# Threshold attention with a feed-forward layer: turning q on VectorE in blocks of 32 from batch 2 on, and spreading inverted sums by DMA

## The chip, the cores and the metric

The kernel runs on one core of a Trainium2 chip. The metric is the device time of one execution in microseconds (us); runs of the same kernel are compared by their median. One execution was taken with the hardware profiler, and its trace is what the views of the profile are read from.

The core's engines run side by side, each through its own instructions in order: TensorE (PE in the profile, with PEld for its weight loads), VectorE (DVE), ScalarE (ACT), GpSimd (POOL) and SyncE (SP). SP computes nothing here; it issues DMAs. An engine waits on semaphores for what another engine or a DMA must have done first.

## The reference

```python
def _attn_ref(q, k, v, tau):                       # q, k, v: 8 batches, 8 heads, 576 tokens, 64
    scale = 1.0 / np.sqrt(q.shape[-1])
    scores = scale * np.matmul(q, k.transpose(0, 1, 3, 2))
    thresh = np.max(scores, axis=-1, keepdims=True) - tau
    scores = np.where(scores >= thresh, scores, -1000000000.0)
    scores = scores - np.max(scores, axis=-1, keepdims=True)
    attn = np.exp(scores)
    attn = attn / (np.sum(attn, axis=-1, keepdims=True) + 1e-09)
    return np.matmul(attn, v).astype(np.float32)

def _moe_ref(x, w_in, w_out):                      # x: 4608 x 512, d_ff = 2048
    h = x @ w_in
    g = np.maximum(0.01 * h, h)
    return (g @ w_out).astype(np.float32)
```

The attention's output, with the heads side by side, is x. Inputs and the output are float32. tau is 0.02, and only scores within tau of the row's maximum count.

## The kernel before

**Tiling.** A *pair* p is two heads of one batch: 32 pairs, four to a batch. A *couple* c is two pairs: 16 couples. A couple's scores are made in nine *steps* t: steps 0 to 3 are 128 query rows each of its first pair, 4 to 7 of its second, and step 8 holds the last 64 rows of both. Each step has two tiles of 128 x 576, one for each head of the pair (h = 0, 1). The program's outer loop goes over 17 values of c and 9 of t, and the last c only finishes the work of couple 15.

**One step.** `s_mm` (L159) makes both score tiles as three fp16 products each (q and k are split into a high part `hi` and a remainder `lo`). They go into the PSUM tag `s`, which has two buffers of two banks, one for each head, so the next step's scores need both to have been read. `s_max` reads a tile with VectorE (L182: scales, negates, takes the minimum, writes `sn`), GpSimd adds tau (L187, `nth`), and then there are two ways to the masked exponentials W. In the plain way ScalarE makes the exponentials `e` (L192), and VectorE masks and sums them (L215, called by `s_mask` a step later). In the *direct* way ScalarE does it all, with two activations (L198, L202). `s_mask` also issues a transposing DMA of W into `wT` from SP (L221). W has six buffers.

**Preparing q and k.** `load_qk` loads a pair's q (L81: one DMA of 256 KB, in pieces of 256 B; L86: the last 64 rows) and k into `nat`, three buffers. `prep(p, i)` turns them so that the 64 head elements lie on partitions: i = 0 is q, four fp32 transposes of 128 x 128 on TensorE (L130) into the PSUM tag `A`; i = 1 is k and both tails, five. ScalarE then copies PSUM to `hi` (L139), and VectorE makes `lo` (L140). Four preparations belong to a couple.

**Sums.** A couple's 18 columns of sums are inverted (`sums_0`, L229; `sums_1`, L235), split into two fp16 parts (L236, and `sums_2`, L241), turned into rows by one product (`sums_3`, L247) and copied by ScalarE (L250). `sums_4` spreads the rows over the partitions of the output tile by products with a selection matrix, five for e = 0 and six for e = 1 (L264), and ScalarE copies each result to `rc` (L269). `values` (L280) multiplies `wT` with v, and VectorE multiplies by `rc` and writes x (L290).

**Feed-forward.** When a batch's x is there, `push_main` puts 32 *units* into a list: 16 of w_in (`h_unit`, L302, each followed by a ScalarE activation, L306) and 16 of w_out (`out_mm`, L317; every fourth is evicted by ScalarE, L328, and every second eviction is followed by a store from SP, L350). The last 64 rows of two batches are collected for `push_tail`, twice four units. The units are independent of the couple in progress and fill TensorE between the other steps.

**Order.** The order within a step is written by hand as a string of words for each t. `share` says which part of the waiting units a step gets, `ahead_of` how many of them run early in the step, and the tiles that go the direct way depend on c, t and whether the step's units hold one of w_in. The instructions of each engine are issued in exactly this order.

Of the kernel before, what the change touches and what calls it, by code (L numbers as in the profile page):

```python
# [9 lines left out]
FP32 = mybir.dt.float32  # L10
# [6 lines left out]
def kernel(  # L17
# [24 lines left out]
    sb = ctx.enter_context(tc.tile_pool(name="sb", bufs=1))  # L42
    ps = ctx.enter_context(tc.tile_pool(name="ps", bufs=1, space=bass.MemoryType.PSUM))
# [29 lines left out]
    def load_qk(p, i, tail):  # L73

        b, g = divmod(p, NG)
        if p not in nat:
            nat[p] = sb.tile([128, 9, 2, 64], FP32, tag="nat", bufs=3, name="nat")
        t = nat[p]
        h2 = (q, k)[i][b, 2 * g:2 * g + 2, :, :]
        if not tail:  # L80
            nc.sync.dma_start(  # L81
                out=t[0:128, 4 * i:4 * i + 4, :, :],
                in_=h2[:, 0:512, :].rearrange("h (p c) d -> p c h d", c=4),
            )
        else:
            nc.sync.dma_start(  # L86
                out=t[ds(64 - 64 * i, 64), 8, :, :],
                in_=h2[:, 512:576, :].rearrange("h p d -> p h d"),
            )
# [22 lines left out]
    due = []  # L112

# [9 lines left out]
    def prep(p, i, tag="A", bufs=1):  # L123
# [3 lines left out]
        pt = pair_of_banks(tag, bufs).rearrange("p a b -> p (a b)")  # L127
        for c in range(4 + i):
# [10 lines left out]
        due.append(lambda: nc.scalar.activation(out=hi[:, :], in_=pt[:, 0:N], func=AF.Copy, bias=0.0, scale=QS))  # L139
        soon.append(lambda: nc.vector.scalar_tensor_tensor(  # L140
            out=lo[:, :], in0=pt[:, 0:N], scalar=QS, in1=hi[:, :],
            op0=OP.mult, op1=OP.subtract,
        ))
        qk.setdefault(p, {})[i] = (hi, lo)

    def s_mm(c, t):
# [17 lines left out]
        sc[(c, t)] = out  # L164

    live, dens = {}, {}

    def s_max(c, t, h, direct):
# [3 lines left out]
        if t == 0 and h == 0:  # L172
            dens[c] = sb.tile([128, 18], FP32, tag="den", bufs=2, name="den")
        if h == 0:
# [20 lines left out]
        else:  # L195
# [8 lines left out]
                accum_out=dens[c][:, 2 * t + h:2 * t + h + 1],  # L204
            )

    def s_mask(c, t):
# [5 lines left out]
        for h in range(2):  # L213
            if h not in masked:
# [3 lines left out]
                    accum_out=dens[c][:, 2 * t + h:2 * t + h + 1],  # L218
                )
        q0 = 512 if t == 8 else t * 128 + (t // 4) * 128  # L220
# [4 lines left out]
    def sums_0(c):  # L225

# [6 lines left out]
    def sums_1(c):  # L233
        d1, rr = inv[c]
        nc.vector.reciprocal(out=rr[:, :], in_=d1[:, :])  # L235
        nc.gpsimd.tensor_scalar(out=r2[:, 0, 0:18], in0=rr[:, :], scalar1=1.0 / RS, scalar2=0.0,  # L236
                                op0=OP.mult, op1=OP.add)

    def sums_2(c):
        d1, rr = inv[c]  # L240
        nc.vector.scalar_tensor_tensor(out=r2[:, 1, 0:18], in0=rr[:, :], scalar=1.0 / RS, in1=r2[:, 0, 0:18],  # L241
                                       op0=OP.mult, op1=OP.subtract)

    def sums_3(c):

# [6 lines left out]

    def sums_4(c, e):

        row = rows[c]
# [12 lines left out]
        rc = sb.tile([128, 576], FP32, tag="rc", bufs=2, name="rc")  # L268
        due.append(lambda: nc.scalar.activation(out=rc[:, :], in_=t[:, 0:576], func=AF.Copy, bias=0.0, scale=1.0))  # L269
        rcs[e] = rc  # L270

    def values(c, e):
# [12 lines left out]
        rc = rcs.pop(e)  # L285
# [3 lines left out]
        def mul():  # L289
            nc.vector.tensor_tensor(  # L290
# [45 lines left out]
    def push_main(b):  # L336

# [3 lines left out]
        for u in range(2):  # L341
# [7 lines left out]
            def store(o, u=u):  # L349
                nc.sync.dma_start(  # L350
                    out=out[ds(b * S, 512), :].rearrange("(p c) n -> p c n", c=4)[:, 2 * u:2 * u + 2, :],
                    in_=o[:, :, :],
                )
# [26 lines left out]
    with tc.manual_schedule():  # L380
# [15 lines left out]
        for p in range(1, 3):  # L396
# [8 lines left out]
        share = (20, 21, 23, 13, 20, 13, 26, 29, 26)  # L405
        ahead_of = (3, 3, 1, 3, -1, 1, 1, 1, -1)

        plain = "scores first units turn_qk evict spread evict second more mask soon"
        before = "scores turn_qk evict first second mask soon"
        orders = {  # L410
            0: "scores turn_qk evict units first second more mask soon",
            1: "scores invert first units rest more second mask soon",
            3: "scores values first units second more mask soon",
            5: "scores first values units second more mask soon",
            6: "scores first turn_qk evict units more second mask soon",
            8: "scores first units turn_qk evict more second mask soon",
        }
# [3 lines left out]
        for c in range(NC + 1):  # L421
            last = c == NC
            for t in range(NT):
                step = c * NT + t
                if c > 1 and c % 2 == 0 and t == 6:

                    if c % 4 == 2 and c > 2:
# [6 lines left out]
                nxt = {6: (2 * c + 2, 0), 7: (2 * c + 2, 1), 8: (2 * c + 3, 0), 0: (2 * c + 1, 1)}  # L434
                if c == 0:
                    nxt[0], nxt[1] = (1, 0), (1, 1)
                pi = nxt.get(t)
                if pi is not None and pi[0] >= NP:
                    pi = None

                ahead = [share[i % NT] for i in range(step, (c // 2 * 2 + (0 if c % 2 == 0 and t < 6 else 2)) * NT + 6)]
                credit = min(credit, 1.0) + (len(units) - credit) * share[t] / sum(ahead)
                n = min(int(credit + 0.01), len(units))
                credit -= n
                n1 = min(n, (n + ahead_of[t]) // 2)
                direct = tau_f <= 16.0 and (
                    t not in (0, 1, 3) if c < 3 else t in (2, 5, 7, 8) or not any(u[0] for u in units[:n]))
                direct0 = tau_f <= 16.0 and c < 3 and t in (0, 3, 5)

                if c == 0 and t < 2 or c < 2 and t == 6:  # L450
                    order = before
                else:
                    order = orders.get(t, plain)
                    if c == 1 and t == 0:
                        order = "scores first turn_qk evict second mask soon"
                for part in order.split():
                    if part == "scores" and not last:
                        s_mm(c, t)
                    elif part == "values" and c > 0:
                        values(c - 1, t // 2 - 1)  # L460
                    elif part == "first" and not last:
                        s_max(c, t, 0, direct0)
                    elif part == "second" and not last:
                        s_max(c, t, 1, direct)
                    elif part == "invert" and c > 0:
                        sums_1(c - 1)
                    elif part == "rest" and c > 0:
                        sums_2(c - 1)
                    elif part == "units":
                        work(n1)  # L470
                    elif part == "more":
                        if c > 0 and t == 1:
                            work(n - n1 - 1)
                            sums_3(c - 1)
                            work(1 if n > n1 else 0)
                        else:
                            work(n - n1)
                    elif part == "turn_qk" and pi is not None:
                        prep(*pi)
                    elif part == "spread" and c > 0 and t in (2, 4):  # L480
                        sums_4(c - 1, t // 2 - 1)
                    elif part == "evict":
# [56 lines left out]
```

## Time and profile before

| | |
|---|---|
| median of 3 runs | 529.51 us (528.81 to 530.55) |
| the profiled execution | 528.58 us |
| its span | 526.8 us |
| mean granted TensorE clock | 0.969 |
| DMA packets, bytes | 266813, 80.50 MB |
| packets under 512 B | 251904 |
| HBM read, written | 36.70 MB, 9.44 MB |

The span is the stretch from the first to the last instruction that was profiled. Busy times of an engine are the union of its instructions; instructions of VectorE and ScalarE overlap their successors by some 0.08 us, so a group's mean is a little more than what one instruction adds. In the lines shown below, L12 is line 12 of the kernel. DMA share is the time that packets took, as a share of 16 DMA engines, summed over the queues, and can pass 1.

### The profile page before, as it was taken

What the parts mean: (1) busy time and instruction counts of PE and PEld (TensorE: products, weight loads), DVE (VectorE), ACT (ScalarE), POOL (GpSimd) and SP (SyncE); (2) the same over time, 40 slices, a digit from 0 to 9 for tenths busy, and PEclk for the clock granted to TensorE, in tenths of its full rate; (3) what the DMA queues carried; (4) which work ended last, traced back from release to release, by engine and by line L of the source; (5) the groups of instructions that cost most, each with busy time, mean ns of one, the idle gap of its engine ahead of it and who ended that gap; (6) DMA issues with size and microseconds to landing.
All of it is one profiled execution on the core that took longest, in us unless ns stands there. A gap on an engine that the chain in (4) does not pass through costs nothing.

```text
span 526.8 us, 12333 instructions
## 1 busy us (share of the span) xinstructions
PE 494.7 (94%) x4384; PEld 272.9 (52%) x4384; DVE 414.7 (79%) x1076; ACT 444.0 (84%) x795; POOL 186.4 (35%) x430
## 2 busy tenths in 40 slices
PE   5577787999999999999999999999999999999996
PEld 3344444555555566555555566555555565545444
DVE  5878887998899888998899888998899888982000
ACT  3896979989999899989898999989898999983622
POOL 0754446543443234323443234323433244321000
PEclk9786969999999999999999999999999999999999
DMA  6999999998997899887999689887998799853011
GB/s 154 137 164 184 205 186 198 206 183 175 164 186 145 152 173 168 167 142 165 183 170 142 150 176 188 146 138 156 189 164 152 147 169 154 116 85 93 40 41 60
DMA packets 266813, 80.50 MB, mean 153 GB/s; under 512 B 251904, under 2 KB 264192, under 8 KB 266752
## 3 DMA queue, kind: packets, MB, share of 16 engines
q1 hardware_dynamic: 249136, 70.68, 75.0%
q0 software_dynamic: 17536, 8.92, 14.8%
q8 instruction: 34, 0.56, 0.5%
q14 instruction: 27, 0.22, 0.1%
q10 hardware_dynamic: 80, 0.13, 0.1%
HBM read 36.70 MB, written 9.44 MB: 88 GB/s over the span
## 4 chain that ended last, share of the span: by engine, by line
PE 83%; ACT 7%; DVE 5%; issue 2%; DMA 2%; POOL 0%; SPq 0%; DVEq 0%; ACTq 0%; POOLq 0%
PE u L317 24%; PE u L302 22%; PE s L159 21%; PE A L280 8%; PE A L130 6%; DVE sn L182 3%; ACT W L202 2%; ACT far L198 2%; ACT e L192 2%; PE A L264 1%; DMA nat<-in_q_dram 1%; DVE W L215 1%; DMA nat<-in_k_dram 1%; ACT hi L139 1%; ACT gM L306 0%
## 5 line engine op out<-in xcount | busy, mean ns | idle before, releaser
L182 DVE TENSOR_SCALAR_CACHE_REDUCE sn<-s 128x576 f32<-128x576 f32 x288 | 207.6, 754 | 41.9 <-PE s L159 40.2
L187 POOL TENSOR_SCALAR nth<-nmx 128x1 f32<-128x1 f32 x288 | 125.6, 436 | 242.2 <-DVE sn L182 219.1
L192 ACT ACTIVATE e<-sn,nmx 128x576 f16<-128x576 f32 x181 | 137.6, 770 | 17.6 <-DVE sn L182 16.4
L215 DVE SCALAR_TENSOR_TENSOR W<-sn,nth,e 128x576 f16<-128x576 f32 x181 | 144.3, 814 | 0.0
L302 PE MATMUL u<-xT,win 128*128 128x512 f16 x512 | 122.7, 380 | 0.4 <-ACT gM L306 0.4
L317 PE MATMUL u<-wout,gM 128*128 128x512 f16 x512 | 122.1, 380 | 0.0
L159 PEld LDWEIGHTS <-hi 64*128 64x128 f16 (+1 forms) x1280 | 65.9, 99 | 70.4 <-issue 53.4
L159 PE MATMUL s<-hi,hi 64*128 64x288 f16 x512 | 87.6, 300 | 11.4 <-DVE sn L182 9.7
L159 PE MATMUL s<-hi,lo 64*128 64x288 f16 (+1 forms) x640 | 93.1, 294 | 0.0
L159 PE MATMUL s<-lo,hi 64*128 64x288 f16 (+1 forms) x640 | 92.8, 293 | 0.0
L198 ACT ACTIVATE far<-sn,nth 128x576 f32<-128x576 f32 x107 | 82.5, 771 | 8.2 <-POOL nth L187 6.3
L302 PEld LDWEIGHTS <-win 128*128 128x128 f16 x768 | 61.2, 98 | 52.5 <-issue 8.4
L202 ACT ACTIVATE W<-far,ntau 128x576 f16<-128x576 f32 x107 | 83.0, 775 | 3.5
L306 ACT ACTIVATE gM<-u 128x512 f16<-128x512 f32 x128 | 71.5, 590 | 6.8 <-PE u L302 6.8
L317 PEld LDWEIGHTS <-gM 128*128 128x128 f16 x512 | 46.5, 98 | 52.6 <-issue 7.9
L140 DVE SCALAR_TENSOR_TENSOR lo<-A,hi 128x512 f16<-128x512 f32 (+1 forms) x63 | 47.6, 755 | 17.0 <-ACT hi L139 16.6
L130 PE MATMUL A<-I,nat 128*128 128x128 f32 x283 | 45.9, 291 | 10.4 <-DVE lo L140 5.1
L139 ACT ACTIVATE hi<-A 128x512 f16<-128x512 f32 (+1 forms) x63 | 40.0, 636 | 10.1 <-PE A L130 10.1
L280 PE MATMUL A<-wT,V 128*64 128x288 f16 x640 | 48.0, 298 | 0.0
L130 PEld LDWEIGHTS A<-I,nat 128*128 128x128 f32 x283 | 32.1, 145 | 26.0 <-DVE lo L140 13.8
L280 PEld LDWEIGHTS <-V 128*64 128x64 f16 x640 | 35.1, 113 | 11.7 <-issue 8.0
L328 ACT ACTIVATE osb<-u 128x512 f32<-128x512 f32 x35 | 20.6, 590 | 23.7 <-PE u L317 23.7
(44 smaller groups left out, 302.8 us busy)
## 6 DMA issues: line engine op xcount, KB each, us to landing
nat<-in_q_dram SPq DMA_DIRECT2D x32, 256.0 KB, 3.6
nat<-in_k_dram SPq DMA_DIRECT2D x32, 256.0 KB, 3.8
out_dram<-osb SPq DMA_DIRECT2D x16, 512.0 KB, 3.6
wT<-W SPq DMA_TRANSPOSE x144, 4.1
V<-in_v_dram POOLq DMA_DIRECT2D x8, 256.0 KB, 5.7
win<-in_moe_w_in_dram POOLq DMA_DIRECT2D x16, 128.0 KB, 5.2
V<-in_v_dram POOLq DMA_DIRECT2D x16, 128.0 KB, 4.9
wout<-in_moe_w_out_dram POOLq DMA_DIRECT2D x16, 128.0 KB, 4.7
```

The source lines that it names most:

```text
L130: nc.tensor.matmul(out=pt[0:128, ds(c * 128, 128)], lhsT=t[0:128, 4 * i + c, :, :].rearrange("p h d -> p (h d)"), rhs=I32[:, :], is_transp ...
L159: nc.tensor.matmul(out=out[h][po, half, 0:288], lhsT=qk[p][i][a][r, cols], rhs=qk[p][1][b][r, ds(half * 288, 288)], start=(ti == 0), stop= ...
L182: nc.vector.tensor_scalar(out=sn[:, h, :].rearrange("p (a b) -> p a b", a=2), in0=s_[:, :, 0:288], scalar1=-BS, scalar2=None, op0=OP.mult, ...
L187: nc.gpsimd.tensor_scalar(out=nth[:, h:h + 1], in0=nmx[:, h:h + 1], scalar1=1.0, scalar2=tau_f, op0=OP.mult, op1=OP.add,)
L192: nc.scalar.activation(out=e[:, h, :], in_=sn[:, h, :], func=AF.Exp, bias=nmx[:, h:h + 1], scale=-1.0,)
L198: nc.scalar.activation(out=far[:, :], in_=sn[:, h, :], func=AF.Prelu, bias=nth[:, h:h + 1], scale=-1.0, alpha=BIG,)
L202: nc.scalar.activation(out=w[:, ds(h * 576, 576)], in_=far[:, :], func=AF.Exp, bias=ntau[:, 0:1], scale=1.0, accum_out=dens[c][:, 2 * t + ...
L215: nc.vector.scalar_tensor_tensor(out=w[:, ds(h * 576, 576)], in0=sn[:, h, :], scalar=nth[:, h:h + 1], in1=e[:, h, :], op0=OP.is_le, op1=OP ...
L280: nc.tensor.matmul(out=t[ds(h * 64, 64), half, 0:288], lhsT=vb[:, g, h, kb, :], rhs=wT[:, 4 * h + kb, ds(e * 576 + half * 288, 288)], star ...
L302: nc.tensor.matmul(out=t[:, ts(j, N)], lhsT=w_in16[:, gi, ts(j0 + j, 128)], rhs=xs[gi], start=(gi == 0), stop=(gi == NG - 1), skip_group_c ...
L306: nc.scalar.activation(out=g_out, in_=t[:, 0:nj * N].rearrange("p (j n) -> p j n", j=nj), func=AF.Prelu, bias=0.0, scale=1.0, alpha=0.01)
L317: nc.tensor.matmul(out=t[:, :], lhsT=g_in(j), rhs=w_out16[:, j, :], start=(j == 0), stop=(j == NJ - 1), skip_group_check=True,)
```

## The change

1. **q of pairs 8 to 31** (batch 2 and later) is loaded by four DMAs of 64 KB, in pieces of 128 B, so that block (h, e) of 32 head elements lies on partitions 64 h + 32 e and after, and 32 rows times 16 token blocks in the free dimension. One VectorE instruction then transposes all 32 x 32 blocks into an SBUF tile `qT`. `hi` and `lo` are made from that tile. The query rows of these pairs come out in another order, and the main stores of batches 2 to 7 undo it: four DMAs for each store of one.
2. **Inverted sums of couples 3 to 14** are turned in fp32 by one TensorE transpose, copied by ScalarE to a tile of 18 x 128, written to DRAM by one DMA (`sums_d`) and read back by four DMAs (`sums_b`), each of which broadcasts one half row of 640 elements over 64 partitions into `rc`. The split into two fp16 parts, the eleven products of `sums_4` and the two copies by ScalarE are left out for them. Couples 0, 1, 2 and 15 keep the products.
3. **New orders**, shares and choices of direct tiles: five lists of nine orders, for c = 0, 1, 2, for odd c from 3 on and for even c from 4 on. In the last two the values stand in steps 5 and 6 instead of 3 and 5, and a batch's units are pushed at step 7 instead of 6.

In the orders S is the scores, 0 and 1 are the tiles' `s_max`, M the mask and transposing DMA of the tile before, U, u and w are units, Pa to Pe are preparations (Pa and Pc are q of the next couple's pairs, Pb and Pd k), h runs the ScalarE copies that are due, L the VectorE work that is due, d, r, x, T, D, R, Q are the steps of the sums (D the row to DRAM, R the broadcast), V is the values, and G pushes units.

```diff
+        if i == 0 and not tail and b >= 2:
+            tq = t[0:128, 0:4, :, :].rearrange("p c h d -> p (c h d)")
+            for h in range(2):
+                for e in range(2):
+                    nc.sync.dma_start(
+                        out=tq[ds(64 * h + 32 * e, 32), :].rearrange("r (b d) -> r b d", d=32),
+                        in_=h2[h, 0:512, ds(32 * e, 32)].rearrange("(r b) d -> r b d", r=32),
+                    )
+            return
...
-        pt = pair_of_banks(tag, bufs).rearrange("p a b -> p (a b)")
-        for c in range(4 + i):
+        turn = i == 1 or p < 2 * NG
+        if turn:
+            pt = pair_of_banks(tag, bufs).rearrange("p a b -> p (a b)")
+        else:
+            pt = sb.tile([128, 512], FP32, tag="qT", bufs=2, name="qT")
+            nc.vector.transpose(
+                out=pt[:, :].rearrange("p (t b r) -> p b t r", t=4, b=4),
+                in_=t[0:128, 0:4, :, :].rearrange("p c h d -> p (c h d)").rearrange("p (b t r) -> p b t r", t=4, b=4),
+            )
+        for c in range(4 + i if turn else 0):
...
+    def by_dma(c):
+        return 3 <= c < 15
...
     def sums_3(c):
+        if by_dma(c):
+            d1, rr = inv[c]
+            t = pair_of_banks().rearrange("p a b -> p (a b)")
+            nc.tensor.matmul(out=t[0:18, 0:128], lhsT=rr[:, :], rhs=I32[:, :], is_transpose=True,
+                             skip_group_check=True)
+            row = sb.tile([18, 128], FP32, tag="row32", bufs=2, name="row32")
+            due.append(lambda: nc.scalar.activation(out=row[:, :], in_=t[0:18, 0:128], func=AF.Copy, bias=0.0, scale=1.0))
+            rows[c] = row
+            return
...
+    def sums_d(c):
+        d = dr.tile([18, 128], FP32, tag="dr", bufs=2, name="dr")
+        nc.sync.dma_start(out=d[:, :], in_=rows[c][:, :])
+        rows[c] = d
+
+    def sums_b(c):
+        d = rows[c]
+        for e in range(2):
+            rc = sb.tile([128, 640], FP32, tag="rc", bufs=2, name="rc")
+            src = d.rearrange("(h i) q -> h (i q)", h=2)[:, ds(512 * e, 640)]
+            for h in range(2):
+                nc.sync.dma_start(out=rc[ds(64 * h, 64), :], in_=src[h:h + 1, :].to_broadcast([64, 640]))
+            rcs[e] = rc[:, ds(64 * e, 576)]
...
+                    for x in range(4):
+                        nc.sync.dma_start(
+                            out=rows_.rearrange("(r x c) n -> x r c n", x=4, c=4)[x, :, 2 * u:2 * u + 2, :],
+                            in_=o[ds(32 * x, 32), :, :],
+                        )
...
-        share = (20, 21, 23, 13, 20, 13, 26, 29, 26)
+        share = (17, 24, 26, 13, 17, 16, 23, 38, 23, 17, 24, 29, 13, 17, 16, 23, 38, 23)
```

The two lists of orders from c = 3 on, one line for each step:

```
odd c                          even c
S Pd h w U 0 h 1 u M d L       S Pd h w U 0 h 1 u M d L
S r 0 U x T u 1 h D w L M      S r 0 U x T u w h D 1 M L
S 0 U Q0 h w u 1 M L R         S 0 U Q0 h w 1 M L u R
S U 0 1 u M L w                S 0 U 1 u w M L
U S 0 Q1 h 1 L M w u           U S 0 Q1 h 1 L M Pa h w u
S V0 0 U w 1 L Pa h M u        S V0 0 U w 1 L M h u
S V1 0 G h U 1 u M L           w S V1 0 h U 1 u M L
S Pc 0 U Pb h 1 u M L          G S Pc 0 U Pb h 1 u M L
S 0 U h u 1 M L w              S 0 U h u 1 M L
```

Q does nothing where the sums go by DMA, and G nothing in odd c. Direct tiles from c = 3 on: h = 0 at step 5 alone; h = 1 at steps 2, 5 and 8, in even c at 3 too, and otherwise, at steps 4 and 6 (in even c 0, 4 and 6), where none of the step's units is of w_in.

## The prediction

> **What bounds the kernel now.** I read the engines' totals first, then the busy time couple by couple, then the chain of waits inside a couple, then the prices, and last the DMA queue of SP. A couple c is 18 score tiles (9 steps); its borders below are the starts of its first `sn`.
>
> ```profile
> PE 494.7 (94%) x4384; PEld 272.9 (52%) x4384; DVE 414.7 (79%) x1076; ACT 444.0 (84%) x795; POOL 186.4 (35%) x430
> ```
>
> The page's totals make TensorE the first suspect, but they average a start, a middle and an end. The table by stage (length, then busy us of PE, PEld, DVE, ACT, POOL, granted clock, DMA share, GB/s) shows couple 2 and then couples 8, 9, 10 and 11:
>
> ```profile
> 65.40:94.78 29.38, 24.23 (x216) 14.37 (x216) 23.94 (x63) 26.28 (x50) 16.61 (x36) 0.85 1.30 196
> 240.60:270.10 29.50, 29.50 (x263) 15.74 (x264) 24.84 (x65) 27.33 (x52) 12.28 (x27) 1.00 1.04 174
> 270.10:299.55 29.45, 29.45 (x263) 15.83 (x264) 26.88 (x70) 26.48 (x47) 8.92 (x22) 1.00 0.83 145
> 299.55:329.11 29.56, 29.56 (x311) 17.92 (x312) 24.84 (x64) 27.50 (x52) 12.27 (x27) 1.00 1.11 190
> 329.11:358.57 29.46, 29.46 (x263) 15.83 (x264) 27.66 (x73) 26.97 (x49) 8.93 (x22) 1.00 0.81 138
> ```
>
> From couple 4 on every couple lasts 29.5 us and PE is busy in all of it. DVE has 4.7 us to spare in even couples but only 1.8 to 2.6 in odd ones, ACT 2.1 to 3.0. So a microsecond off PE is a microsecond off the time only until DVE's spare time is used up, and the change gives DVE more work. In couples 0 to 2 no engine is full. The chain of waits inside couples 8 and 9 prices the PE work (start, us, piece):
>
> ```profile
> 252.65 0.36 PE A L264 x6
> ...
> 259.60 0.58 PE A L130 x4
> ...
> 266.85 0.64 PE A L130 x4
> ...
> 275.16 0.06 PE A L247
> ...
> 277.02 0.25 PE A L264 x5
> ```
>
> L130 x4 is the turn of one q, L264 x5 and x6 the two spreads of a couple, L247 the turn of the sums.
>
> **PE.** By the change's conditions q is turned on DVE for pairs 8 to 31, 24 turns: 24 x 0.60 = 14.4 us leave PE. The spreads of couples 3 to 14 go: 12 x (0.36 + 0.25) = 7.3 us. The turn of the sums becomes an fp32 transpose, 0.15 (a quarter of 0.60) for 0.06: 12 x 0.09 = 1.1 us come back. The net is 20.6 us. A couple from 4 to 14 would need 29.49 - 1.20 - 0.61 + 0.09 = 27.8 us of PE. The profiled execution took 528.58 us (span 526.8, 1.8 around it), so with PE always fed it would take 508.0. The Trainium skill (VectorE: DVE Perf Modes, The three transpose paths) gives 390 ns for one 128x128 TensorE transpose and 311 ns for VectorE; 96 at 390 ns would be an estimated 37 us. The chain shows 0.15 us each, and the trace decides.
>
> **DVE, ACT.** The prices, with mean ns of one:
>
> ```profile
> L140 DVE SCALAR_TENSOR_TENSOR lo<-A,hi 128x512 f16<-128x512 f32 x32 | 22.0, 688 | 6.3 <-ACT hi L139 6.0
> L192 ACT ACTIVATE e<-sn,nmx 128x576 f16<-128x576 f32 x181 | 137.6, 770 | 17.6 <-DVE sn L182 16.4
> L269 ACT ACTIVATE rc<-A 128x576 f32<-128x576 f32 x32 | 20.3, 633 | 0.8 <-PE A L264 0.8
> L139 ACT ACTIVATE hi<-A 128x512 f16<-128x512 f32 x32 | 18.6, 580 | 6.9 <-PE A L130 6.9
> ```
>
> No block transpose is in this trace. It streams 512 fp32 elements, as `lo` does in 0.69; a 128x256 copy at 0.43 is the low end, two passes over `lo`'s elements (0.69 + 0.53) = 1.2 the high end. I take 0.69, the same element count, twice a couple: 1.4. The remainder `r` of L241 goes (-0.17). Worked through step by step, the loop's own planning lowers the tiles whose mask ACT makes (`direct`) from 107 (the x107 of L202) to 102, in couples 4 to 14 from 8 to 7 in 6, 10 and 14. Each moves one W of 0.74 net (0.81 less its overlap with the next instruction) to DVE, 0.4 per even couple. DVE then needs 24.84 + 1.4 - 0.17 + 0.4 = 26.4 us in even couples, and (26.88 + 27.66)/2 + 1.4 - 0.17 = 28.5 us in odd ones, against 27.8 of PE. ACT loses two `rc` evictions, 1.27 a couple. `hi` of q now reads SBUF instead of PSUM: rows of 576 from SBUF cost 0.770 (e), from PSUM 0.633 (rc), so +0.14 twice. ACT ends near 26 us and isn't the bound.
>
> So the even couples stay with PE, and in the odd ones DVE takes over. PE may start the next step's scores only when both `sn` of this step have left PSUM, and DVE's next `sn` waits for those scores (0.84 us). DVE covers them with its masks, `lo` and `xT`, but at step 5 both tiles are now direct, so little is left to cover the next scores. The fullest DVE in this trace is couple 3 (26.91 of 28.22 us, 95%, with PE at 99%). I take 97 to 98% for a DVE that is the bound: 28.5 becomes 29.2, a gain of 0.3 us in an odd couple; in even ones 0.2 us of waiting leaves 1.5. Sum: couples 4 to 14, 6 x 1.5 + 5 x 0.3 = 10.5. Couple 3 gets two DVE turns and one direct tile less (26.91 + 1.4 + 0.7 = 29.0 on 28.2): -0.8. Couple 15 has no preparation left and saves the spread alone: +0.5. That is 10.2 us: 518.4.
>
> **Start and end.** The orders of couples 0 to 2 are new as well. A step of couple 0 is 2.92 us, two `sn` of 0.76 and scores of 1.40 at a granted clock of 0.75, and no order shortens that. Couples 1 and 2 last 29.2 and 29.4, 6 us in all above nine such steps each; I count zero and keep 3 us either way. After 480 us only PE works: couple 15's sums are spread by products as before, values come at steps 5 and 6 for 3 and 5, with older units left to fill: zero, at worst the 0.9 us of one unit.
>
> **SP and the DMA engines.** Here the change adds most. From couple 4 to 14 SP spends 20.6 us per couple in issuing (sum over its DMA instructions in the trace):
>
> ```profile
> 260.51 2.10 SPq L221 DMA_TRANSPOSE wT<-W  x1
> 262.66 0.63 SPq L86 DMA_DIRECT2D nat<-in_q_dram  x1
> 263.38 1.33 SPq L221 DMA_TRANSPOSE wT<-W  x1
> 264.76 0.63 SPq L81 DMA_DIRECT2D nat<-in_k_dram  x1
> ```
>
> An issue costs 0.6, a store 0.36 (its median). Each q load becomes four: 2 x 3 x 0.62 = 3.7. The row to DRAM is one issue, its broadcast four: 3.0. Each main store becomes four, one store a couple: 3 x 0.36 = 1.1. That is 28.4 us of a couple of 28.5. It is this full only if a transpose keeps its mean of 1.64; the shortest take 1.3, and the longer ones follow loads still being moved, which the engines would finish while SP issues small DMAs. At 1.3 it is 25.3. On the engines, a q load goes from 1024 packets of 256 B to 2048 of 128 B; in the trace's packets 256 B take 24 ns and 2048 and 4096 B 101 and 178, so the split adds between nothing and 1024 x 24 / 16 = 1.5 us per q, and the broadcast 256 x 120 / 16 = 1.9 us per couple. From a mean share of 0.93 (27.5 us) that comes to at most 32.5 of 28.5, a share of 1.14. Couple 2 ran at 1.30, with SP issuing 26.2 of its 29.4 us, and from 9 to 100 us PE's waits for a DMA come to under 1 us. So I count nothing here, because W has six buffers, loads run nine steps ahead, and the values are put off by one to two steps. What waits newly on SP is the broadcast, for the row's landing in DRAM (3.6 us for stores). Two transposes, a load and the step between cover about 3 us; queued behind it are a load and the next transposes.
>
> **Rivals.** First, PE stays fed in odd couples too, because a DVE turn is shorter than `lo` (0.43 would make odd couples 28.0). Then the sum is the PE sum, 508. For it: PE did not wait in couples 7 and 11 with DVE at 94%. Against it: 28.5 is more than 27.8.
>
> Second, DVE takes nearly all of it: a turn costs 1.2, or DVE gets no further than 95%. Odd couples take 29.6 to 30.0, even ones 28.2, about 5 x 0.3 lost against 6 x 1.3 won: 523 to 527. For it: nothing in this trace passes 95%.
>
> Third, slower: SP becomes the bound. It decides when its issues and waits pass 29.5 us per couple. With 28.4 of issues at the present mean, and 1 to 2 us in which it stands at the broadcast for the row's landing, a couple is 29.4 to 30.4; the later transposes keep W's buffers, ACT and DVE stop, then PE. At 30.4 it is 11 x 0.9 = 10 us over: 538. For it: SP issued 28.96 of 29.22 us in couple 1. Against it: PE did not wait for DMAs there, and small DMAs should shorten the transposes. The Trainium skill (DMA: Bandwidth & Descriptors, Rules for kernel authors) says to merge small transfers, since under 64 KB mostly overhead is paid. The rows speak half for that rule here: a 32 KB load costs SP the same 0.6 as a 256 KB one.
>
> **The numbers.** The forecast of 518.4 (512 to 523) has 0.50, the full PE gain (505 to 512) 0.17, DVE taking nearly all (523 to 529) 0.14, SP bound (530 to 540) 0.15, and 0.04 is for an order that makes an engine wait where I see none, slower. A measurement of this kernel can tell about 0.3%, 1.6 us, from no change; of the second rival about half lies below that. The median of the runs lies 0.9 us above the profiled execution, within that bound. Faster 0.73, same 0.07, slower 0.20. The range of 507 to 532 leaves out the best of the first rival and most of the third.
>
> **What would show it.** Right: even couples near 28, odd ones near 29, with DVE over 96% busy and PE waiting for `sn` in odd couples; a row of 24 DVE transposes near 0.69; L264 down to 44 products. Wrong: PE busy throughout and couples of 27.8 all alike; or PE waiting at L280 for `wT`, and SP issuing without a gap; or transposes over 1 us.

## The result, and the profile after

The changed kernel takes 556.38 us (median of 4 runs, 553.7 to 561.44) against 529.16 us of the kernel before (4 runs beside it, 528.5 to 530.55): a ratio of 1.0536, with a 95% interval of 1.0503 to 1.0569. It is 5.4% slower; the forecast was 518.4. Its profiled execution took 556.83 us, with a span of 555.1.

The page's totals, the counterpart of the first line shown of before:

```profile
PE 496.2 (89%) x4156; PEld 268.3 (48%) x4156; DVE 425.9 (77%) x1098; ACT 426.8 (77%) x761; POOL 176.1 (32%) x418
```

There are 228 products fewer and 17 us less of ACT, DVE has risen by only 11 us, and yet every share has fallen: no engine that computes is the bound. Going by the first `sn` of each couple, couples 0 to 2 cost 1.4 us more than before, couples 3 to 14 25.3 more and what follows 1.6 more. The table by stage (columns as before) for couples 9, 10 and 13:

```profile
285.50:314.23 28.73, 28.44 (x245) 14.60 (x244) 27.34 (x74) 25.40 (x46) 8.13 (x22) 1.00 0.81 158
314.23:350.36 36.13, 31.57 (x295) 19.47 (x293) 26.28 (x68) 25.56 (x47) 11.39 (x26) 0.91 1.00 175
415.12:443.51 28.39, 28.11 (x244) 14.32 (x243) 27.42 (x72) 25.18 (x46) 7.74 (x22) 1.00 0.90 166
```

Couples are now unequal. Couple 13 is over a microsecond faster than the 29.46 of before, and couple 10 is 6.6 us slower, with PE idle for 4.6 us of it and VectorE for 9.9. DMA engines are hardly fuller than before (a share of 0.81 to 1.04 in couples 4 to 14, 0.95 on average; 0.71 to 1.11 and 0.94 before). The table of waits (us in total, times, longest) and the chain that ended last name the place:

```profile
DVE xT L365 <- DMA rc<-dr: 26.2, 8, 5.3
```

```profile
PE u L377 16%; PE u L392 15%; PE s L182 12%; DVE sn L216 8%; DMA rc<-dr 8%; PE A L352 5%; DVE W L249 4%; ACT e L226 2%; PE A L149 2%; SPq L320 2%; DVE qT L143 1%; DVE xT L365 1%; ACT far L232 1%; ACT W L236 1%; DMA nat<-in_q_dram 1%
```

VectorE stands at `xT` (L365) until the broadcast inverted sums have landed. In couples 4 to 14 it is idle for 32.5 us ahead of `xT`, 2.95 a couple, where before it was not idle there at all. (5.3 of these are at the second `xT` of a couple, 1.7 of them for the broadcast as well.) Behind it in VectorE's order stand the next mask and `sn`, so GpSimd, ScalarE and TensorE follow. In couple 10, SP's queue (start, us, piece) shows why the sums of couple 9 are late. Their row was in SBUF at 319.44:

```profile
317.57 1.93 SPq L434 DMA_DIRECT2D out_dram<-osb  x4
319.60 1.49 SPq L256 DMA_TRANSPOSE wT<-W  x1
321.19 3.67 SPq L85 DMA_DIRECT2D nat<-in_q_dram  x4
324.96 0.48 SPq L310 DMA_DIRECT2D dr<-row  x1
...
329.09 2.48 SPq L320 DMA_DIRECT2D rc<-dr  x4
```

The row left 5.5 us after it was made: the last of four stores, a transpose and a q load in four pieces stood ahead of it. The broadcasts were issued 4.1 us after the row, right behind the two transposes and the load that come between, and the wait for them on VectorE was over at 335.29:

```profile
329.59 0.69 DVE L161 SCALAR_TENSOR_TENSOR lo<-qT,hi 128x512 f16<-128x512 f32 x1 [0.27 <-ACT hi L158]
335.29 0.76 DVE L365 TENSOR_TENSOR xT<-A,rc 128x576 f16<-128x576 f32 x1 [5.01 <-DMA rc<-dr]
```

In couple 13 the row of couple 12 was ready at 421.70 and SP was free:

```profile
421.72 0.30 SPq L310 DMA_DIRECT2D dr<-row  x1
...
425.63 2.51 SPq L320 DMA_DIRECT2D rc<-dr  x4
```

`xT` ran at 430.29 without a wait, 8.6 us after the row. That is all the time an odd couple's order leaves; an even couple leaves 10.8 us (from 319.44 to 330.28). From the row's issue to the first broadcast's took 3.4 to 6.2 us, and from there to a recorded landing 3 to 6 us. A row that leaves a few microseconds late is thus too late.

SP had no time to catch up. In its timeline the pauses of more than 0.2 us between one DMA's end and the next one's start come to 3.5 us in all of couples 4 to 14; before they came to 87.9.

### The profile page after: what moved, and what is told of

It is laid out like the page before. It is cut to its first block, busy times and chain, and to the rows that moved or that the text cites. A ratio compares the mean times of both kernels' runs of the same rounds, so it can differ in the third digit from the quotient of the medians.

```text
span 555.1 us, 12030 instructions
## 1 busy us (share of the span) xinstructions
PE 496.2 (89%) x4156; PEld 268.3 (48%) x4156; DVE 425.9 (77%) x1098; ACT 426.8 (77%) x761; POOL 176.1 (32%) x418
## 4 chain that ended last, share of the span: by engine, by line
PE 50%; DVE 16%; DMA 10%; ACT 6%; issue 5%; SPq 3%; POOL 1%; DVEq 0%; POOLq 0%; ACTq 0%
PE u L377 16%; PE u L392 15%; PE s L182 12%; DVE sn L216 8%; DMA rc<-dr 8%; PE A L352 5%; DVE W L249 4%; ACT e L226 2%; PE A L149 2%; SPq L320 2%; DVE qT L143 1%; DVE xT L365 1%; ACT far L232 1%; ACT W L236 1%; DMA nat<-in_q_dram 1%
## 5 line engine op out<-in xcount | busy, mean ns | idle before, releaser
L221 POOL TENSOR_SCALAR nth<-nmx 128x1 f32<-128x1 f32 x288 | 114.7, 398 | 258.1 <-DVE sn L216 249.5
L182 PE MATMUL s<-hi,hi 64*128 64x288 f16 x512 | 94.1, 297 | 17.2 <-DVE sn L216 15.3
L182 PEld LDWEIGHTS <-hi 64*128 64x128 f16 (+1 forms) x1280 | 70.6, 99 | 69.2 <-issue 51.9
L236 ACT ACTIVATE W<-far,ntau 128x576 f16<-128x576 f32 x102 | 79.1, 775 | 3.3
L352 PE MATMUL A<-wT,V 128*64 128x288 f16 x640 | 54.2, 323 | 19.9 <-DVE xT L365 17.8
L365 DVE TENSOR_TENSOR xT<-A,rc 128x576 f16<-128x576 f32 x32 | 24.2, 756 | 44.7 <-DMA rc<-dr 26.2
L352 PEld LDWEIGHTS <-V 128*64 128x64 f16 x640 | 40.8, 122 | 31.2 <-issue 25.7
L182 PEld LDWEIGHTS <-lo 64*128 64x128 f16 (+1 forms) x640 | 34.3, 99 | 22.2 <-issue 18.4
L149 PE MATMUL A<-I,nat 128*128 128x128 f32 x187 | 30.6, 297 | 8.0 <-DMA nat<-in_q_dram 4.4
L161 DVE SCALAR_TENSOR_TENSOR lo<-A,hi 128x640 f16<-128x640 f32 (+1 forms) x39 | 30.9, 793 | 5.5 <-ACT hi L158 5.4
```

The lines of the kernel that those rows point to most:

```text
L149: nc.tensor.matmul(out=pt[0:128, ds(c * 128, 128)], lhsT=t[0:128, 4 * i + c, :, :].rearrange("p h d -> p (h d)"), rhs=I32[:, :], is_transp ...
L182: nc.tensor.matmul(out=out[h][po, half, 0:288], lhsT=qk[p][i][a][r, cols], rhs=qk[p][1][b][r, ds(half * 288, 288)], start=(ti == 0), stop= ...
L221: nc.gpsimd.tensor_scalar(out=nth[:, h:h + 1], in0=nmx[:, h:h + 1], scalar1=1.0, scalar2=tau_f, op0=OP.mult, op1=OP.add,)
L236: nc.scalar.activation(out=w[:, ds(h * 576, 576)], in_=far[:, :], func=AF.Exp, bias=ntau[:, 0:1], scale=1.0, accum_out=dens[c][:, col(c, t ...
L352: nc.tensor.matmul(out=t[ds(h * 64, 64), half, 0:288], lhsT=vb[:, g, h, kb, :], rhs=wT[:, 4 * h + kb, ds(e * 576 + half * 288, 288)], star ...
```

## The experiments

**The theories**, under the letters that the expectations use. S: SP's queue is too full once both parts are in. It issues 20.6 us per couple before and 29.3 of 31.75 us after (18.3 and 30.9 DMAs a couple), so the row and its broadcast, which are wanted within some ten microseconds, are issued late. L: the spread by DMA is too slow in itself, whatever else SP does. B: the new orders are to blame, or VectorE has too much work.

The runs are called e1 to e15, as marked below. e2, e3 and e10 leave out the blocked layout of q, the order of the output rows, or both, so what they compute is not the attention; they show what time the rest takes and are no kernels to use.

**One part undone.** Products again for all couples, with q on VectorE and the new orders kept (e1):

```diff
-        return 3 <= c < 15
+        return False
```

> All couples keep the products for the inverted sums; q on VectorE with its four loads and four stores, and the orders, stay. If the late broadcast makes the stall at step 5 (theory S, SP's queue; theory L, the round trip through DRAM itself), the stall goes in both: couples 4 to 14 fall from a mean of 31.8 to about 28.8 us and the time from 556 to about 523. If instead the new orders or a full VectorE make it (theory B), couples stay near 31 and the time near 550.

It took 529.57 us, 1.0006 (0.9985 to 1.0027) of before. All of the loss is gone with the new orders and VectorE's turns still in, so theory B falls as its cause. But the gain that q's turn was to bring (523 was expected) is not there either. Couples 9 and 10 of it:

```profile
266.84:296.00 29.16, 28.59 (x255) 14.87 (x254) 27.71 (x75) 26.43 (x48) 8.01 (x23) 1.00 0.87 151
296.00:325.53 29.53, 29.10 (x305) 17.33 (x304) 26.54 (x71) 26.37 (x49) 11.64 (x27) 1.00 1.01 167
```

PE is no longer full. Its score products take 8.54 us a couple against 8.23 before, and PE stands 0.24 us a couple ahead of them, most of it for `sn`, where it did not stand before.

The other half: q by one DMA, as before the change, with the spread by DMA kept (e2):

```diff
-            for h in range(2):
-                for e in range(2):
...
+            nc.sync.dma_start(
+                out=t[0:128, 0:4, :, :],
+                in_=h2[:, 0:512, :].rearrange("h (p c) d -> p c h d", c=4),
+            )
```

> Left out: the blocked layout of q. Each q is loaded by one DMA of 256 KB in natural order, and VectorE transposes those bytes just the same; the rest is as changed. SP issues six DMAs fewer per couple (3.7 us and more). Theory S: the row goes to DRAM as soon as ScalarE has made it, xT waits under 1 us, couples near 28.8, time 523 to 530. Theory L: the wait of xT for the broadcast stays at 3 to 5 us in even couples, time above 545. Theory B: no change, 550 and more.

It took 529.07, 1.0015 (0.9983 to 1.0047). Six issues fewer in a couple bring nearly all of the loss back, with the spread by DMA in place: L falls. The edit changes more than the number, since a q load is also in pieces of 256 B again. Not all waits are gone, and couples 4 to 14 take 29.48 us on average, not the 28.8 expected:

```profile
DVE xT L362 <- DMA rc<-dr: 8.3, 4, 3.8
```

Then the stores, in one piece (e3):

```diff
-                if b < 2:
+                if True:
```

> Left out: the order of the output rows. Main stores are one DMA each again, the rest is as changed. SP issues six DMAs fewer per batch, 1.1 us a couple, and the four of a store no longer stand ahead of the row in even couples (1.9 us). Theory S: the stalls of even couples shrink by 1.5 to 2 us, time 540 to 548. Theories L and B: 553 to 557.

550.83, 1.0372 (1.0302 to 1.0441), with runs from 544.29 to 552.82. Three issues fewer bring back between a fifth and a third of the loss, less than theory S had expected. With one load and one store together (e10):

> Left out: the blocked layout of q and the order of the output rows. One load for each q and one for each store, broadcasts by SP, the rest as changed: SP issues 4.8 us less per couple. If SP's fill is what makes row and broadcast late: xT's waits are under 0.5 us in nearly all couples, mean couple 28.4 to 28.8, time 519 to 524. If crowded DMA engines hold the broadcast up: waits of 2 us and more stay in odd couples, time 527 to 530.

525.38, 0.9899 (0.9837 to 0.996): 1% less than before, and between the two times expected, as some waits stay in odd couples (5.5 us ahead of `xT` in couples 4 to 14). SP pauses for 21.9 us there. Its couples 9 and 10 show what the change is worth where SP keeps up:

```profile
271.54:299.94 28.40, 28.12 (x244) 14.35 (x243) 27.43 (x74) 25.29 (x46) 8.16 (x22) 1.00 0.94 184
299.94:328.99 29.05, 28.61 (x294) 16.80 (x293) 26.36 (x70) 25.44 (x47) 11.43 (x26) 1.00 1.05 187
```

**The load without the change.** If the number of DMAs is enough, they slow the old kernel too, with no row to wait for. The q loads and stores of before in four pieces, and five DMAs a couple whose data nobody reads, in the row's and the broadcasts' sizes (the pieces of q are of 64 KB as in the change, but of 256 B and not 128 B; e11):

```diff
+        if not tail and i == 0 and b >= 2:
+            for c in range(4):
+                nc.sync.dma_start(
+                    out=t[0:128, c, :, :],
+                    in_=h2[:, 0:512, :].rearrange("h (p c) d -> p c h d", c=4)[:, c, :, :],
+                )
...
+                for x in range(1 if b < 2 else 4):
...
+                if 4 <= c < 16 and t == 1:
...
+                    nc.sync.dma_start(out=x[:, :], in_=moe_w_in[0:18, 0:128])
+                if 4 <= c < 16 and t == 2:
+                    for e in range(2):
...
+                        for h in range(2):
+                            nc.sync.dma_start(out=x[ds(64 * h, 64), :], in_=moe_w_in[ds(64 * h, 64), ds(640 * e, 640)])
```

> The kernel of before, its result unchanged, with SP's load of the changed one: each q load of pairs 8 to 31 and each main store from batch 2 on in four DMAs, and in couples 4 to 15 one DMA of 9 KB and four of 160 KB more, read into tiles that nobody uses. Nothing that an engine waits for within a couple stands in SP's queue. If SP is the bound by the sum of its issues, whatever they carry: couples of 30.5 and more, time above 540. If its fill matters only through the broadcast, which is wanted within ten us: 529 to 532.

538.54, 1.0156 (1.0101 to 1.021), between the two times expected. SP issues 28.1 us of a couple of 30.5 and pauses for 4.0 us in couples 4 to 14. The waits are where the third rival had put them, at the values for the transposed W:

```profile
PE A L286 <- DMA wT<-W: 10.0, 8, 3.0
```

Each half of it alone (the split loads and stores, e13; the five DMAs, e14):

> The kernel of before with q loads of pairs 8 to 31 and main stores from batch 2 on in four DMAs each, nothing more. If the number of issues alone made the 8 us of the run with all of the load: 534 to 538. If the bytes of the broadcasts did: 528 to 531.

> The kernel of before with the five further DMAs of couples 4 to 15 alone, read into tiles that nobody uses. If the number of issues counts: 529 to 531, since these are five of thirteen more. If their bytes, queued ahead of the transposes, do: 533 to 538. If only both together pass a limit: both kernels 528 to 532.

The split loads and stores took 529.72, 1.0028 (0.9996 to 1.0059), the five DMAs 528.86, 1.0012 (0.9991 to 1.0033). Neither costs anything that can be told; together they cost 1.6%. With either alone SP issues 23.9 or 25.8 us a couple and still pauses for 44.7 or 23.8 us. That is how a queue with a limit behaves, not a price for each DMA.

**Other places for the DMAs.** The row and the broadcasts from ScalarE's queue (e5):

```diff
-        nc.sync.dma_start(out=d[:, :], in_=rows[c][:, :])
+        nc.scalar.dma_start(out=d[:, :], in_=rows[c][:, :])
...
-                nc.sync.dma_start(out=rc[ds(64 * h, 64), :], in_=src[h:h + 1, :].to_broadcast([64, 640]))
+                nc.scalar.dma_start(out=rc[ds(64 * h, 64), :], in_=src[h:h + 1, :].to_broadcast([64, 640]))
```

> Nothing left out: the row's DMA and the four broadcasts are issued by ScalarE instead of SP, at the same places in the order; all loads, stores, packets and engine work are as changed. Theory S (SP's queue reaches row and broadcast too late): the row leaves as soon as it is made, the waits of xT for the broadcast fall under 1 us, time 525 to 533. Theory L (the round trip or crowded DMA engines): the landings stay as late, time above 545.

554.34, 1.0472 (1.0444 to 1.0499). The row leaves at once and `xT` waits only 2.7 us in couples 4 to 14, but now ScalarE waits. Its timeline in couple 4 and the waits of the whole:

```profile
129.67 0.56 ACTq L310 DMA_DIRECT2D dr<-row  x1
...
132.81 0.51 ACTq L320 DMA_DIRECT2D rc<-dr  x1
...
134.10 0.45 ACTq L320 DMA_DIRECT2D rc<-dr  x1
...
136.70 0.45 ACTq L320 DMA_DIRECT2D rc<-dr  x1
...
138.36 0.45 ACTq L320 DMA_DIRECT2D rc<-dr  x1
138.86 0.78 ACT L226 ACTIVATE e<-sn,nmx 128x576 f16<-128x576 f32 x1 [5.24 <-DMA nat<-in_q_dram]
```

```profile
DVE W L249 <- issue: 21.0, 8, 5.2
PE u L377 <- ACT gM L381: 18.3, 7, 5.4
```

No broadcast takes ScalarE longer than usual, but it stands between them, and the next `e` behind them, with ScalarE idle for 5.24 us. The trace shows what it stood for. The program's DMAs share a few semaphores in turn, and each is issued only when the last DMA on its semaphore has landed. The second to fourth broadcast were issued 0.02 us after a transpose (134.08) and two pieces of a q load (136.68, 138.34) of SP's had landed. Such waits for SP's transposes and q loads come to some 10 us in couples 4 to 14. So this run ties ScalarE to SP's DMAs; it does not price the place of the queue. SP's issuing fell by only 0.8 us a couple (29.34 to 28.51), though five DMAs worth 2.8 us (0.47 + 4 x 0.59) had left it: its transposes grew from 1.75 to 1.88 us on average. The Trainium skill (DMA: Bandwidth & Descriptors, Issuing engines are not separate DMA queues) says that issuing from several engines saves only the time to initiate, as all run on the same DMA engines. Here less than that was saved, 0.8 of 2.8 us; whether the DMA engines are why is not shown.

The q loads from GpSimd, one piece a step (e12):

```diff
-                nc.sync.dma_start(
+                nc.gpsimd.dma_start(
```

> Nothing left out: the four loads of each q of pairs 8 to 31 are issued by GpSimd, one in each step, and SP keeps all else, 23 to 24 us of issues a couple. Theory S: row and broadcast are in time, waits of xT under 1 us, and the time is that of the version with one load, 522 to 529. If GpSimd's issues delay nth, ScalarE waits for nth in the direct tiles: 530 to 538.

539.14, 1.0173 (1.011 to 1.0237). SP issues 26.2 us a couple, about as little as with the products, and pauses for 23.8 us in couples 4 to 14, but the row is still 3.5 to 4.4 us late in couples 5, 7 and 11, and `xT` idles 18.7 us in all. Couple 3 takes 34.65 us for 28.41, waiting for a transposed W. Here the number of issues on SP does not explain the whole: its transposes take 1.96 us on average. GpSimd's own busy time rose to 242.2 us, but ScalarE's waits for `nth` in the direct tiles stayed at 23.2 us (22.0 in the changed kernel), so that rival falls.

Pair 2c+3's loads in the reverse order, so that its k comes ahead of its q (e4):

```diff
-                    load_qk(2 * c + 3, t // 2, t % 2)
+                    load_qk(2 * c + 3, 1 - t // 2, 1 - t % 2)
```

> Nothing left out, and the same number of issues: in steps 0 to 3 the loads of the next pair go in the reverse order (k's tail, k, q's tail, q), so the four loads of q stand behind the broadcast and not ahead of the row. Theory S, by lateness: the row leaves 2 to 3 us earlier, the stall of even couples falls from 4 to 5 us to about 1 or 2, time 530 to 540. Theory S, by SP's total alone (issues fill the couple whatever their order), and theory L: 550 to 557.

557.6, 1.0561 (1.051 to 1.0612). The idle time ahead of `xT` falls from 32.5 to 22.0 us, but couple 3 begins at 99.74 us instead of 96.13, and couples 4 to 14 still take 31.29 on average: no gain, as theory S by SP's total had it (550 to 557). SP pauses for 3.5 us, as in the changed kernel.

The loads of v, all in the even couples, spread over odd and even ones (e15):

```diff
-                if c % 2 == 0 and c > 0 and t >= 4 and c // 2 < B:
-                    load_v(c // 2, t - 4)
+                if c == 2 and t >= 4:
+                    load_v(1, t - 4)
+                if c > 2 and (c + 1) // 2 < B + (c % 2 == 0):
+                    i = {(1, 4): 0, (1, 6): 1, (1, 8): 2, (0, 1): 3, (0, 3): 4}.get((c % 2, t))
+                    if i is not None and (c + 1) // 2 < B:
+                        load_v((c + 1) // 2, i)
```

> The changed kernel, nothing left out: from batch 2 on the five v loads go from steps 4 to 8 of a batch's first couple to steps 4, 6 and 8 of the couple before and 1 and 3 of its own. If v's bytes slow the transposes and so put SP behind for the next couple's row: the waits of xT fall by half or more, time 532 to 545. If the number of SP's issues is enough by itself: 550 to 558.

556.98, 1.0516 (1.0463 to 1.0569). The lateness moved to the odd couples (35.9 and 35.7 us for couples 9 and 11) and stayed as large (39.0 us ahead of `xT`): where v's transfers lie does not decide how much is lost. Nor is it shown that it decides which couple is late: in e2 and e12, with v's loads where they were, the late rows are in odd couples too.

**The orders.** q on VectorE alone on the orders of before (loads, turn and stores as in the change, not shown), with q's turn behind the second `sn` of steps 6 and 8 (e6), and then the new orders with both parts undone (e7; the stores in one piece and the moved turns are not shown):

```diff
+                    if c > 2 and t in (6, 8):
+                        order = "scores first units second turn_qk evict more mask soon"
```

> Part 1 alone, on the kernel of before and its orders: q of pairs 8 to 31 turned on VectorE (behind the step's second sn, at steps 6 and 8), four loads, four stores; products for all sums, values at steps 3 and 5. TensorE loses 1.0 us per couple. If TensorE stays the bound: couples near 28.6, time 517 to 522. If VectorE, now fuller, makes TensorE wait for sn as it did with the products kept in the changed kernel: couples near 29.3, time 526 to 531.

```diff
-        if i == 0 and not tail and b >= 2:
+        if False:
...
-        turn = i == 1 or p < 2 * NG
+        turn = True
...
-        return 3 <= c < 15
+        return False
```

> Part 3 alone: the new orders with q turned on TensorE by one load, one store, and products for all sums (q's turns moved to steps 6 and 8, since they need the PSUM buffer of the values). If the new orders cost nothing by themselves: 527 to 531. If values in two neighbouring steps and units moved away from them make engines wait: 533 to 540, with TensorE waiting for sn in steps 0 to 4.

They took 550.42, 1.041 (1.0354 to 1.0466), and 547.06, 1.0343 (1.0318 to 1.0368). Both fell to my own placement of q's turn. In the first, `lo` waits for `hi` in the same step (38.9 us in all) and steps 6 and 8 of couples 9 and 10 last 4.6 us for 3.15. In the second, TensorE's turn had to move, since it needs a buffer of `A`, and `lo` waits 34.5 us. They say nothing on the two parts, except that a preparation needs a step between its pieces.

Products (as in e1), new orders, and the values back in steps 3 and 5 (odd c shown, even c alike; e8):

```diff
-'S U 0 1 u M L w'
+'S V0 0 U 1 u M L w'
...
-'S V0 0 U w 1 L Pa h M u', 'S V1 0 G h U 1 u M L'
+'S V1 0 U w 1 L Pa h M u', 'S 0 G h U 1 u M L'
```

> Products kept for all sums, q on VectorE, the new orders but the values back at steps 3 and 5 (from couple 3 on). Against 529.6 with the values at 5 and 6. If the late, neighbouring values eat the gain of the lighter TensorE: 519 to 525. If it is VectorE's fill alone: 528 to 531.

532.45, 1.007 (1.0044 to 1.0095): the later values are not what e1 loses by.

Last, the first part alone on the orders of before, with VectorE's turn at the end of steps 5 and 7, `hi` in the next step and `lo` at its end (e9):

```diff
+                    if c > 2:
+                        order = {5: order + " turn_q", 6: "scores first evict units more second mask soon",
+                                 7: order + " turn_q", 8: "scores first units evict more second mask soon"}.get(t, order)
...
+                    elif part == "turn_q":
+                        if 2 * c + 2 + t // 7 < NP:
+                            prep(2 * c + 2 + t // 7, 0)
```

> Part 1 alone on the orders of before, arranged as the changed kernel does it: VectorE turns q at the end of steps 5 and 7, ScalarE makes hi in the step after, and VectorE lo at that step's end, so no engine stands for the next. Products for all sums. If the 20 us of the first try came from where the turn stood: couples near 28.6 to 29, time 518 to 525. If a fuller VectorE or SP takes the gain by itself: 527 to 535.

522.76 (521.25 to 525.83) against 530.1, 0.9864 (0.9804 to 0.9923): it beats both kernels, by 1.4% the one before. Couples 9 and 10:

```profile
267.20:296.26 29.06, 28.91 (x258) 15.39 (x257) 27.65 (x74) 26.22 (x48) 9.09 (x23) 1.00 0.92 163
296.26:324.95 28.69, 28.54 (x303) 16.77 (x301) 25.51 (x67) 27.23 (x51) 12.05 (x27) 1.00 0.99 177
```

PE is fed again, SP issues 26.0 us a couple, and no `xT` waits for a DMA. q comes in four pieces of 128 B here, so the pieces and the four loads cost less than VectorE's turn saves. Against e1, which has the same part on the new orders, it is some 7 us less: with the products kept, the new orders cost the gain.

**What is shown, and what stays open.** Shown: the loss needs both parts (e1, e2 and e10; e13 and e14 against e11 show the same of the DMAs alone), and it enters at the wait for `rc`, whose row and broadcasts stand behind other issues on an SP that does not pause. Open: how much of SP's lateness is the number of issues and how much the length of its transposes. e2, e10 and e12 keep some late rows with fewer issues on SP, and the transposes' mean moves between 1.55 and 1.96 us from kernel to kernel without following the issues. What in the new orders costs e1 its gain was not found; e8 rules out the place of the values alone. The row and its broadcasts placed ahead of SP's loads, with fewer pieces, were not tried. Nor does any run show the spread by DMA to pay: e10, where SP keeps up, leaves out layout and row order and is still no faster than e9 with the products.

## Why the prediction was wrong

**The step that failed** is the one on SP and the DMA engines, at "So I count nothing here". It put the whole of SP's load at nothing. The runs show in its place a queue without pauses, rows that leave up to 5.75 us late, and VectorE idle for 32.5 us at `xT` in couples 4 to 14. The step's sum was good: 28.4 us of issues a couple were forecast, 29.3 measured. It failed in three readings of that sum.

1. The slack it named, W's six buffers, loads nine steps ahead and values put off, belongs to transposes and loads. It set no clock for the row. From row to `xT` there are 8.6 to 10.8 us, and 7 to 9 of them go until a broadcast has landed even where the row is issued at once (in e10 from 278.15 to 285.22, and from 305.26 to 314.15). Of these, 3.9 and 4.9 us pass before the first broadcast is issued, while SP issues two transposes and a load.
2. "Two transposes, a load and the step between cover about 3 us" asked what SP does while the row lands. That much held: SP never stood there, as each first broadcast was issued within 0.1 us of the end of the DMA ahead of it. But it took for granted that the row is issued when it is made. It left up to 5.75 us late.
3. That couple 2 ran with SP at 26.2 of 29.4 us, and couple 1 at 28.96 of 29.22, showed only that transposes and loads can be late; the kernel before sends no row.

The forecast that small DMAs would shorten the transposes to 1.3 us was wrong as well: their mean in couples 4 to 14 went from 1.60 (1.64 was taken) to 1.75.

**The third rival** had the right engine and sign, at 0.15. Its place was wrong: it looked for the wait at L280 for `wT`, which is what e11 shows, and here it is at `xT` for `rc`. Its price was too small: 30.4 us a couple against 31.75, since it charged SP's excess over a couple and not the standing of all engines behind one late row. The 1 to 2 us in which SP was to stand for the row's landing did not come.

**The sum.** Against the profiled execution, 518.4 was forecast. The idle time at `xT` adds 32.5. Without it couples 4 to 14 take 28.79 on average, (349.23 - 32.5) / 11, where the forecast had 28.51: 3.1 more. Couple 3 took 28.41 for 29.0: 0.6 less. The start was 1.4 more, and the end 1.6 more where 0.5 less was forecast: 2.1. That is 556.9; 556.83 was measured. The 28.79 is what is left over, so that the sum comes out says nothing of causes. One of them is likely the granted clock: it was 0.90 to 0.95 in couples 5, 6, 8, 10 and 12, the five of 33 us and more, and 1.00 in the others of couples 4 to 14. PE was busy for 324.6 us in couples 4 to 14, and for 312.2 in e10 with the same products. No run shows why the clock fell just there. So but for the waits the forecast was some 6 us off, and e10, with one load and one store, took 525.4.

**Right terms.** VectorE's turn of q, and the two groups that read it (us in all, mean ns):

```profile
L143 DVE STREAM_TRANSPOSE qT<-nat 128x512 f32<-128x512 f32 x24 | 16.9, 703 | 0.0
L161 DVE SCALAR_TENSOR_TENSOR lo<-qT,hi 128x512 f16<-128x512 f32 x24 | 16.6, 690 | 4.7 <-ACT hi L158 4.7
L158 ACT ACTIVATE hi<-qT 128x512 f16<-128x512 f32 x24 | 14.8, 616 | 2.8 <-DVE qT L143 2.8
L336 PE MATMUL A<-row,sel 128*128 128x128 f16 x28 | 3.5, 253 | 1.3 <-ACT row L304 1.3
L336 PE MATMUL A<-row,sel 128*128 128x64 f16 x16 | 2.7, 209 | 0.0
```

A turn takes 0.70 us for the 0.69 taken, so the second rival's 1.2 falls; the spreads are down to 28 + 16 = 44. VectorE gets to 97% (27.43 of 28.40 us in couple 9 of e10), past the 95% that was the second rival's other leg. Odd couples of e9 take 29.05 to 29.28, near the 29.2 forecast, but e9 keeps the products and the orders of before, so that is no test of it.

**Mis-sized terms.** Even couples were to take 28.0 and odd ones 29.2; in e10 they take some 29.05 and 28.4 where no row is late, so even and odd are exchanged. That the mean is nearly kept, 28.49 without the idle time at `xT` for 28.51, is luck. VectorE's work in couple 9 went from 26.88 us to 27.43, by 0.55 where 1.2 was forecast; why so little is open. In e10's couple 10 PE is busy for 28.61 us, for 27.8: one turn of q is worth 0.50 us on PE, not 0.60 (in couples 4 to 13, from the start of each product to that of the next, TensorE's turns took 21.3 us before and 11.3 in e10), and the score products take 0.36 us a couple more (8.59 against 8.23) and wait for `sn` in the even couples too, not only in the odd. `hi` from SBUF costs 0.03 us more than from PSUM (0.616 against 0.588), not 0.14; ACT wasn't the bound.

The Trainium skill's rule to merge transfers (DMA: Bandwidth & Descriptors, Rules for kernel authors), of which the prediction said that the rows speak half for it, decides here in one sense only. Pieces of 64 KB lie at that rule's border. Four for one cost nothing measurable while SP has room (e13, 1.0028, in pieces of 256 B), and with pieces of 128 B e9 is still faster than the kernel before. Once SP has no room, four loads and four stores for one of each cost 31 us (556.4 against 525.4 in e10).

## What to carry to other kernels

Sum the issues of a DMA queue as for any engine, but do not ask only whether they fit: ask which of them has a deadline, count the time from when its data are made to when they are used, and subtract every trip and everything queued ahead. Two edits that each fit in an engine's slack can fail together, so an edit with several parts should be tried part by part; here one part on the orders of before is 1.4% faster, and both together 5.4% slower. A small transfer through DRAM that replaces a few cheap products on a full engine needs an issuing queue with room at the right moment; that it pays even then is not shown here. And a DMA moved to another engine's queue can still wait for the old queue's DMAs, if the program shares semaphores between them.

## What the runs showed of the hardware

- A 64 KB load in pieces of 128 B takes SP as long to issue as one of 256 KB in pieces of 256 B (0.63 and 0.64 us median for q). For the same bytes it takes the DMA engines 17% longer: a 128 B packet took 13.7 ns, a 256 B packet 23.5. So the split costs issues above all.
- A 9 KB row written to DRAM can be read again 3.4 us after its issue (sums of couple 14), and 2.8 us in e5. In the changed kernel SP did not stand for it even there, so this is a bound from above and not the length of the trip.
- A transposing DMA holds SP for 1.24 us at the least, 1.41 in the median and 5.55 at the most, and the long ones come in other places when other DMAs are moved.
- A broadcast of 160 KB issued from ScalarE takes it 0.55 us in the median and 1.20 at the most (e5), as from SP (0.59); the longer stands of ScalarE in e5 lie between the issues.
- In the changed kernel the granted clock was 0.90 to 0.95 in the five couples of 33 us and more, and 1.00 in the other six of couples 4 to 14.
